# Attention backward: each dV product and each dK product also carries a transpose

## Chip, cores and metric

One core of one Trainium2 chip. The metric is the device time of one execution in microseconds; the kernel before takes 1630.79 us (median of 3 runs, 1629.3 to 1632.03).

## The reference

Two independent attention blocks A and B share the incoming gradient; the kernel computes the forward output and all gradients. B = 8 batches, Sq = 96 queries, H = 32 heads, Dh = 128, Sk = 512 cached keys, model width D = 640, all bf16.

```
def _A_ref(x, k_cache, v_cache, wq, wo):          # _B_ref is the same
    q = (x @ wq).reshape(B, Sq, H, Dh).transpose(0, 2, 1, 3)
    scores = jnp.einsum("bhqd,bhkd->bhqk", q, k_cache) * (Dh ** -0.5)
    p = softmax(scores, axis=-1)
    o = jnp.einsum("bhqk,bhkd->bhqd", p, v_cache)
    return o.transpose(0, 2, 1, 3).reshape(B, Sq, H * Dh) @ wo

def reference(..., grad_out):
    out, vjp = jax.vjp(concat(A, B), all ten inputs)
    return (out, *vjp(grad_out))   # dx, dk_cache, dv_cache, dwq, dwo of A and of B
```

Per head and batch: dV = P^T dO, dP = dO V^T, delta = rowsum(dO * O), dS = P * (dP - delta), dK = dS^T Q, dQ = dS K.

## The kernel before

The kernel is unrolled over blocks, heads and batches: 2 x 32 x 8 = 512 pairs of head and batch, and each pair passes through a software pipeline of "ticks", one pair entering per tick. Within a tick every stage stands in a slot; the list of (tick, slot) is sorted and emitted, and the framework's scheduler then fixes each engine's order, its buffers and its waits (`high_priority` moves the score path forward). One tick holds, each for another pair:

- s8 (`c_s8`): dQ^T in four products of 96 columns into `x_ps`, from `K_sb` and `dST_sb`; then, for the pair of s7, four transposes of dS into `dst_ps` (L349) and the DVE copy to `dST_sb` (L351).
- s7 (`c_s7`): dK in four products of 128 columns, `dS_sb` stationary and `Qnat_h` moving (L435), evacuated by ACT to `dK_sb` (L438).
- s5 and s4 (`c_s45`): O^T in four products into `x_ps` (L362), four transposes of P into `x_ps` (L368), ACT evacuations to `OD` (L378) and `PT_sb` (L381).
- s4 (`c_s4`): dV in four products, `P_sb` stationary and `dOnat_h` moving (L392), evacuated by ACT to `dV_sb` (L395).
- s6 (`c_s6`): dP (L420), the row sums delta as a product of `prod` and a column of ones into `dl_ps` (L422), and dS on DVE in one instruction (L424).
- s2, s3: scores `S_ps` (L301), their maximum on DVE (L303), exp on ACT (L313), reciprocal on DVE (L323), P on GpSimd (L332). s5b: `prod` on GpSimd (L410).

s4 to s8 of one pair follow each other tick by tick, so dST of a tick is read by dQ^T in the next, PT by O^T in the next, and dS by dK in the next.

Work by head (projections `q_ps` L246, transposes of weights, `n_ps` L261 for Q and dO in natural layout, `nat_ps` L458, weight gradients `dwo_ps` L472 and `dwq_ps` L493, output and dx products `o_ps` L517) is placed at the end of ticks, with evacuations on ACT or DVE through the helper `evac` (L160, L163, L165). SyncE issues the loads, the DMA transposes of K and V, and the stores.

PSUM has eight banks here, in one pool, and each tile takes one:

```
ps=P(name="ps", bufs=8, space=PSUM),
...
def bank(shape, dt, name):
    return ps.tile(shape, dt, name=name, tag="bank")
```

Of the kernel before, what the change touches and what calls it, by code (L numbers as in the profile page):

```python
# [7 lines left out]
ACT = mybir.ActivationFunctionType  # L8
ALU = mybir.AluOpType
AX = mybir.AxisListType  # L10
F32 = mybir.dt.float32
BF16 = mybir.dt.bfloat16
PSUM = bass.MemoryType.PSUM
# [33 lines left out]
OFF = dict(ldk=-5, ldv=-4, kt=-3, vt=0, s2=3, s3=3, s4=4, s5=5, s6=6, s7=7, s8=8)  # L47
HK = dict(pA=-10, pA2=-9, pB=-3, pC0=[-2, 0], pC1=[-1, 0], pD1=1, pD0=2, qA0=18, qA1=17, qA1e=21, qDw=(18, 29), qB=[19, 20], qD=[(18, 0, 2), (19, 2, 4), (21, 4, 5)])
EV = dict(pB0="act", pB1="dve", pC00="act", pC01="act", pC10="act", pC11="dve", pD0="dve", pD1="dve", qA0="act", qA1="dve", qB0="act", qB1="dve", qD="dve", gU="act")
# [4 lines left out]
SLOTS = dict(LOAD=0, S2A=5, S2B=5.5, S1=6, S8=10, S7=20, S5=30, S4=40, S6=50, S3A=52, S3B=53, S5B=54, HEAD=SL_HEAD, GRP=SL_GRP)  # L54


def build_block(tc, em, tick0, blk, x, kc, vc, wq, wo, g_all, out_all, dx, dk, dv, dwq, dwo, ident, ones, pools, HG=6, first=True, groups=None):
    nc = tc.nc
    B, Sq, D = x.shape
    _, H, Sk, Dh = kc.shape  # L60
# [40 lines left out]
    def bank(shape, dt, name):  # L101
        return ps.tile(shape, dt, name=name, tag="bank")
# [3 lines left out]
    SB = {}  # L106
# [51 lines left out]
    def evac(eng, dst, src, sc=None):  # L158
        if eng == "act":
            nc.scalar.activation(dst, src, ACT.Identity, scale=(1.0 if sc is None else sc))  # L160
        else:
            if sc is None:
                nc.vector.tensor_copy(dst, src)  # L163
            else:
                nc.vector.tensor_scalar(dst, src, float(sc), None, op0=ALU.mult)  # L165
# [84 lines left out]
    def pD(h, which):  # L250
        def f():
            st = HS[(blk, h)]
            src = st["QT_h"] if which == 0 else st["dOT_h"]
            dst = hd.tile([Sq, B * 128], BF16, name="Qnat_h" if which == 0 else "dOnat_h")
            st["Qnat_h" if which == 0 else "dOnat_h"] = dst
            for b0 in range(0, B, 8):
                nb = min(8, B - b0)
                n_ps = bank([Sq, 8 * 128], BF16, "n_ps")
                for i in range(nb):
                    b = b0 + i  # L260
                    nc.tensor.transpose(n_ps[:, i * 128:(i + 1) * 128], src[:, b * Sq:(b + 1) * Sq], ident[:])  # L261
                evac(EV["pD%d" % which], dst[:, b0 * 128:(b0 + nb) * 128], n_ps[:, 0:nb * 128])
        return f

    def c_ld(h, b, n, bufs):
# [70 lines left out]
    def c_s8(tick, k8, k7):  # L336
        def f():
            XP[tick] = bank([128, 1024], BF16, "x_ps")
            if k8 is not None:
                st = CS[(k8[0], k8[1], k8[2])]  # L340
                dQT_ps = XP[tick][:, 2 * Sq:4 * Sq].bitcast(F32)
                for c in range(KC):
                    nc.tensor.matmul(dQT_ps, st["K_sb"][:, c, :], st["dST_sb"][:, c * Sq:(c + 1) * Sq], start=(c == 0), stop=(c == KC - 1))  # L343
                del CS[(k8[0], k8[1], k8[2])]
            if k7 is not None:
                st7 = CS[(k7[0], k7[1], k7[2])]
                dST_ps = bank([128, KC * Sq], BF16, "dst_ps")
                for c in range(KC):
                    nc.tensor.transpose(dST_ps[:, c * Sq:(c + 1) * Sq], st7["dS_sb"][:, c * 128:(c + 1) * 128], ident[0:Sq, 0:Sq])  # L349
                dST_sb = wk.tile([128, KC * Sq], BF16, name="dST_sb", bufs=2)  # L350
                nc.vector.tensor_copy(dST_sb[:], dST_ps[:])  # L351
                st7["dST_sb"] = dST_sb
        return f

    def c_s45(tick, k8, k5, k4):
        def f():
            pt_ps = XP.pop(tick)
            if k5 is not None:
                st = CS[(k5[0], k5[1], k5[2])]
                OT_ps = pt_ps[:, 0:2 * Sq].bitcast(F32)  # L360
                for c in range(KC):
                    nc.tensor.matmul(OT_ps, st["V_sb"][:, c, :], st["PT_sb"][:, c * Sq:(c + 1) * Sq], start=(c == 0), stop=(c == KC - 1))  # L362
            if k4 is not None:
                st4 = CS[(k4[0], k4[1], k4[2])]
                P_sb = st4["P_sb"]
                PT_ps = pt_ps[:, 4 * Sq:4 * Sq + KC * Sq]
                for c in range(KC):
                    nc.tensor.transpose(PT_ps[:, c * Sq:(c + 1) * Sq], P_sb[:, c * 128:(c + 1) * 128], ident[0:Sq, 0:Sq])  # L368
            both = [(k, which) for which, k in enumerate((k5, k8)) if k is not None]
            if both:  # L370
                at = [(HS[(k[0], k[1])]["slot"], k[2] * Sq) for k, _ in both]
                v = OD[:, both[0][1], at[0][0], at[0][1]:at[0][1] + Sq]
                src = pt_ps[:, 2 * Sq * both[0][1]:2 * Sq * (both[-1][1] + 1)].bitcast(F32)
                if len(both) == 2:
                    step = (OD.shape[2] + at[1][0] - at[0][0]) * T + at[1][1] - at[0][1]
                    v = bass.AP(v.tensor, v.offset, [v.ap[0], (step, 2), (1, Sq)])
                    src = src.rearrange("p (a q) -> p a q", a=2)
                nc.scalar.activation(v, src, ACT.Identity, scale=1.0)  # L378
            if k4 is not None:
                PT_sb = wk.tile([128, KC * Sq], BF16, name="PT_sb", bufs=2)  # L380
                nc.scalar.activation(PT_sb[:], PT_ps, ACT.Identity, scale=1.0)  # L381
                st4["PT_sb"] = PT_sb
        return f

    def c_s4(h, b):
        def f():
            st = CS[(blk, h, b)]
            hs = HS[(blk, h)]
            P_sb = st["P_sb"]
            dV_ps = bank([128, KC * 128], F32, "dV_ps")  # L390
            for c in range(KC):
                nc.tensor.matmul(dV_ps[:, c * 128:(c + 1) * 128], P_sb[:, c * 128:(c + 1) * 128], hs["dOnat_h"][:, b * 128:(b + 1) * 128], start=True, stop=True)  # L392
            if b % 2 == 0:
                SB[(blk, h, b // 2, "v")] = wk.tile([128, 2, KC * 128], BF16, name="dV_sb", bufs=4)
            nc.scalar.activation(SB[(blk, h, b // 2, "v")][:, b % 2], dV_ps[:], ACT.Identity, scale=1.0)  # L395
        return f

    def c_st(h, b, which):
# [5 lines left out]
    def c_s5b(h, b):  # L404
# [6 lines left out]
            st["prod"] = prod  # L411
        return f

    def c_s6(h, b):
        def f():
            st = CS[(blk, h, b)]
            hs = HS[(blk, h)]
            tok = slice(b * Sq, (b + 1) * Sq)
            dP_ps = bank([Sq, Sk], F32, "dP_ps")
            nc.tensor.matmul(dP_ps[:], hs["dOT_h"][:, tok], st["VT"], start=True, stop=True)  # L420
            dl_ps = bank([Sq, 1], F32, "dl_ps")
            nc.tensor.matmul(dl_ps[:], st["prod"][:], ones[:, 0:1], start=True, stop=True)  # L422
            dS_sb = wk.tile([Sq, Sk], BF16, name="dS_sb", bufs=2)
            nc.vector.scalar_tensor_tensor(dS_sb[:], dP_ps[:], dl_ps[:, 0:1], st["P_sb"][:], op0=ALU.subtract, op1=ALU.mult)  # L424
            st["dS_sb"] = dS_sb
        return f

    def c_s7(h, b):
        def f():
            st = CS[(blk, h, b)]  # L430
            hs = HS[(blk, h)]
            dS_sb = st["dS_sb"]
            dK_ps = bank([128, KC * 128], F32, "dK_ps")
            for c in range(KC):
                nc.tensor.matmul(dK_ps[:, c * 128:(c + 1) * 128], dS_sb[:, c * 128:(c + 1) * 128], hs["Qnat_h"][:, b * 128:(b + 1) * 128], start=True, stop=True)  # L435
            if b % 2 == 0:
                SB[(blk, h, b // 2, "k")] = wk.tile([128, 2, KC * 128], BF16, name="dK_sb", bufs=4)
            nc.scalar.activation(SB[(blk, h, b // 2, "k")][:, b % 2], dK_ps[:], ACT.Identity, scale=1.0)  # L438
        return f

    def qA(h, which):
# [121 lines left out]
    for g in range(NG):  # L563
        h0 = GH0[g]
        for hh in range(groups[g]):
# [17 lines left out]
            for b in range(B):  # L583
# [14 lines left out]
                if b % 2 == 1:  # L598
                    em.add(ct + OFF["s4"] + 1, SLOTS["LOAD"] + 1.5, c_st(h, b, "v"))
                    em.add(ct + OFF["s7"] + 1, SLOTS["LOAD"] + 1.5, c_st(h, b, "k"))  # L600
                em.add(ct + OFF["s4"], SLOTS["S4"], c_s4(h, b))
                for i, o in enumerate(("s8", "s7", "s5", "s4")):
                    SX.setdefault(ct + OFF[o], [None] * 4)[i] = (blk, h, b)
                em.add(ct + OFF["s6"], SLOTS["S6"], c_s6(h, b))
                em.add(ct + OFF["s7"], SLOTS["S7"], c_s7(h, b))
            hk = HK if first or h < H - 1 else dict(HK, qA0=13, qB=[14, 15], qA1=16, qD=[(19, 0, 2), (19, 2, 4), (19, 4, 5)])
# [42 lines left out]
def _kernel_impl(tc, A_x, A_k_cache, A_v_cache, A_wq, A_wo, B_x, B_k_cache, B_v_cache, B_wq, B_wo, grad_out,  # L649
# [13 lines left out]
    with ExitStack() as ctx:  # L663
# [7 lines left out]
        nc.vector.memset(warm[:], 1.0)  # L671
        pools = dict(
            const=P(name="const", bufs=1),
            ps=P(name="ps", bufs=8, space=PSUM),
            kvp=P(name="kv", bufs=11),
            wk=P(name="wk", bufs=3),
            hd=P(name="hd", bufs=2),
# [7 lines left out]
        pools["SX"] = {}  # L685
        pools["XP"] = {}
        pools["OD"] = pools["const"].tile([128, 2, HG + 2, A_x.shape[0] * A_x.shape[1]], BF16, name="OD", bufs=1)
        pools["HS"] = {}
        pools["CS"] = {}
        em = Emitter()  # L690
# [77 lines left out]
```

## Time and profile before

| | |
|---|---|
| median of 3 runs | 1630.79 us |
| profiled execution | 1629.74 us, its span 1628.0 us |
| TensorE (PE) busy | 1605.0 us, 99% of the span, 20881 matmuls |
| TensorE weight loads (PEld) | 1286.4 us, 79% |
| VectorE (DVE) | 1269.9 us, 78% |
| ScalarE (ACT) | 1391.5 us, 85% |
| GpSimd (POOL) | 528.5 us, 32% |
| granted TensorE clock | 0.999 |
| DMA | 454.96 MB, mean 279 GB/s |

PE is the matmul stream, PEld the weight loads that run beside it. A group line of the profile gives line, engine, operation, what is written and read with shapes, the count, then busy time in us, mean ns of one, idle time before it and what ended that. A timeline line gives start and length in us. Matmuls are pipelined, so the length of one is not what it costs in a stream; the distance of starts is.

### The profile page before, as it was taken

Reading aid. Unit: us, or ns where it says so; the run is one execution under the profiler, and the core shown is the slowest. Engines: PE = TensorE matmul, PEld = TensorE weight load, DVE = VectorE, ACT = ScalarE, POOL = GpSimd, SP = SyncE. Lnnn points to the kernel's source line nnn. Section 1 sums busy time; section 2 is a strip of 40 time slices with the busy share of each in tenths; the row PEclk is TensorE's granted clock in tenths of the full one; section 3 lists DMA queues with packets and bytes.
Section 4 is the critical chain, followed back from the end, with each engine's and each line's share of the span. In section 5 each row is a group of like instructions: output and inputs, shape, how many; then the busy total and the mean of one; then the engine's idle time right before and its main releaser. Section 6 shows DMA issues by size and latency. Waiting matters only on the chain.

```text
span 1628.0 us, 55048 instructions
## 1 busy us (share of the span) xinstructions
PE 1605.0 (99%) x20881; PEld 1286.4 (79%) x21048; DVE 1269.9 (78%) x2907; ACT 1391.5 (85%) x3518; POOL 528.5 (32%) x1034
## 2 busy tenths in 40 slices
PE   8999999999999999999999999999999999999998
PEld 7887787787788787877878777877877877877876
DVE  6886687778788788788878767878878878777887
ACT  7999898798898797988879889978987977987984
POOL 2333333233333233333323323323333333332332
PEclk9999999999999999999999999999999999999999
DMA  9999999999999999999999999999999999999994
GB/s 268 284 290 293 274 292 285 278 275 289 283 281 287 274 282 278 272 277 299 277 303 287 285 285 286 283 294 277 276 295 268 294 288 266 283 274 285 287 280 142
DMA packets 875626, 454.96 MB, mean 279 GB/s; under 512 B 548192, under 2 KB 875360, under 8 KB 875360
## 3 DMA queue, kind: packets, MB, share of 16 engines
q1 hardware_dynamic: 875360, 451.43, 112.8%
q8 instruction: 165, 2.70, 0.7%
q14 instruction: 101, 0.83, 0.1%
HBM read 161.09 MB, written 159.12 MB: 197 GB/s over the span
## 4 chain that ended last, share of the span: by engine, by line
PE 93%; DVE 2%; ACT 2%; issue 1%; DMA 1%; SPq 0%; POOL 0%; DVEq 0%; ACTq 0%; POOLq 0%
PE q_ps L246 13%; PE o_ps L517 12%; PE dK_ps L435 7%; PE dV_ps L392 7%; PE dP_ps L420 7%; PE S_ps L301 7%; PE dwo_ps L472 6%; PE dwq_ps L493 6%; PE dst_ps L349 5%; PE x_ps L368 5%; PE x_ps L362 5%; PE x_ps L343 5%; PE n_ps L261 3%; PE nat_ps L458 3%; PE woT_ps L213 1%
## 5 line engine op out<-in xcount | busy, mean ns | idle before, releaser
L332 POOL TENSOR_SCALAR P_sb<-E_sb,rinv 96x512 bf16<-96x512 bf16 x512 | 354.2, 692 | 1072.2 <-DVE rinv L323 1038.4
L313 ACT ACTIVATE E_sb<-S_ps,negm 96x512 bf16<-96x512 f32 x512 | 356.3, 696 | 117.2 <-DVE negm L303 111.7
L424 DVE SCALAR_TENSOR_TENSOR dS_sb<-dP_ps,dl_ps,P_sb 96x512 bf16<-96x512 f32 x512 | 382.8, 748 | 43.6 <-PE dl_ps L422 36.6
L438 ACT ACTIVATE dK_sb<-dK_ps 128x512 bf16<-128x512 f32 x512 | 307.4, 600 | 84.8 <-PE dK_ps L435 83.8
L303 DVE TENSOR_REDUCE negm<-S_ps 96x1 f32<-96x512 f32 x512 | 347.6, 679 | 37.5 <-PE S_ps L301 36.4
L395 ACT ACTIVATE dV_sb<-dV_ps 128x512 bf16<-128x512 f32 x512 | 316.2, 618 | 0.0
L381 ACT ACTIVATE PT_sb<-x_ps 128x384 bf16<-128x384 bf16 x512 | 258.1, 504 | 0.0
L517 PEld LDWEIGHTS <-OD 128*128 128x128 bf16 x1536 | 135.3, 98 | 102.8 <-issue 2.0
L392 PE MATMUL dV_ps<-dOnat_h,P_sb 96*128 96x128 bf16 x2048 | 197.9, 219 | 0.6 <-DVE dOnat_h L163 0.6
L435 PE MATMUL dK_ps<-Qnat_h,dS_sb 96*128 96x128 bf16 x2048 | 198.0, 219 | 0.0
L420 PE MATMUL dP_ps<-VT,dOT_h 128*96 128x512 bf16 x512 | 195.3, 381 | 0.3
L323 DVE RECIPROCAL rinv<-rowsum 96x1 f32<-96x1 f32 x512 | 80.3, 157 | 144.8 <-ACT E_sb L313 141.5
L351 DVE COPY dST_sb<-dst_ps 128x384 bf16<-128x384 bf16 x512 | 177.7, 347 | 17.5 <-PE dst_ps L349 17.5
L410 POOL TENSOR_TENSOR prod<-OD,dOT_h 128x96 bf16<-128x96 bf16 x512 | 186.5, 364 | 8.8 <-ACT OD L378 8.2
L301 PE MATMUL S_ps<-KT,QT_h 128*96 128x512 bf16 x488 | 184.9, 379 | 0.4
L378 ACT ACTIVATE OD<-x_ps 128x192 bf16<-128x192 f32 (+1 forms) x515 | 173.3, 336 | 3.7 <-PE x_ps L343 3.7
L349 PE MATMUL dst_ps<-ident,dS_sb 96*128 96x96 bf16 x2048 | 172.4, 206 | 0.5 <-ACT PT_sb L381 0.3
L362 PE MATMUL x_ps<-PT_sb,V_sb 128*128 128x96 bf16 x2048 | 172.2, 206 | 0.2 <-ACT PT_sb L381 0.2
L368 PE MATMUL x_ps<-ident,P_sb 96*128 96x96 bf16 x2048 | 171.9, 205 | 0.6 <-POOL P_sb L332 0.3
L343 PE MATMUL x_ps<-dST_sb,K_sb 128*128 128x96 bf16 x2048 | 170.9, 206 | 0.0
L343 PEld LDWEIGHTS <-K_sb 128*128 128x128 bf16 x2048 | 135.3, 98 | 38.2
L493 PE MATMUL dwq_ps<-dQnat,x_nat 128*128 128x256 bf16 x960 | 142.7, 273 | 0.0
(75 smaller groups left out, 3042.5 us busy)
## 6 DMA issues: line engine op xcount, KB each, us to landing
out_dram<-dV_sb SPq DMA_DIRECT2D x256, 256.0 KB, 3.6
out_dram<-dK_sb SPq DMA_DIRECT2D x256, 256.0 KB, 3.5
K_sb<-in_A_k_cache_dram SPq DMA_DIRECT2D x128, 256.0 KB, 4.1
V_sb<-in_A_v_cache_dram SPq DMA_DIRECT2D x128, 256.0 KB, 3.9
K_sb<-in_B_k_cache_dram SPq DMA_DIRECT2D x128, 256.0 KB, 4.0
V_sb<-in_B_v_cache_dram SPq DMA_DIRECT2D x128, 256.0 KB, 4.0
out_dram<-dwo_sb SPq DMA_DIRECT2D x64, 160.0 KB, 3.2
out_dram<-dwq_sb SPq DMA_DIRECT2D x32, 320.0 KB, 4.2
```

Source lines behind the costliest of these rows:

```text
L301: nc.tensor.matmul(S_ps[:], hs["QT_h"][:, tok], st["KT"], start=True, stop=True)
L303: nc.vector.tensor_reduce(negm[:], S_ps[:], axis=AX.X, op=ALU.max, negate=True)
L313: nc.scalar.activation(E_sb[:], st["S_ps"][:], ACT.Exp, bias=st["negm"][:], scale=1.0, accum_out=rowsum[:])
L332: pinned(nc.gpsimd.tensor_scalar(P_sb[:], st["E_sb"][:], st["rinv"][:], 0.0, op0=ALU.mult, op1=ALU.add))
L343: nc.tensor.matmul(dQT_ps, st["K_sb"][:, c, :], st["dST_sb"][:, c * Sq:(c + 1) * Sq], start=(c == 0), stop=(c == KC - 1))
L392: nc.tensor.matmul(dV_ps[:, c * 128:(c + 1) * 128], P_sb[:, c * 128:(c + 1) * 128], hs["dOnat_h"][:, b * 128:(b + 1) * 128], start=True, s ...
L395: nc.scalar.activation(SB[(blk, h, b // 2, "v")][:, b % 2], dV_ps[:], ACT.Identity, scale=1.0)
L420: nc.tensor.matmul(dP_ps[:], hs["dOT_h"][:, tok], st["VT"], start=True, stop=True)
L424: nc.vector.scalar_tensor_tensor(dS_sb[:], dP_ps[:], dl_ps[:, 0:1], st["P_sb"][:], op0=ALU.subtract, op1=ALU.mult)
L435: nc.tensor.matmul(dK_ps[:, c * 128:(c + 1) * 128], dS_sb[:, c * 128:(c + 1) * 128], hs["Qnat_h"][:, b * 128:(b + 1) * 128], start=True, s ...
L438: nc.scalar.activation(SB[(blk, h, b // 2, "k")][:, b % 2], dK_ps[:], ACT.Identity, scale=1.0)
L517: nc.tensor.matmul(o_ps[:], src[:, t * 128:(t + 1) * 128], rhs, start=(hh == 0), stop=(hh == groups[g] - 1))
```

## The change

The four transposes of P and the four dV products have the same stationary operand, a chunk of P; likewise dS and dK. The change puts the 96 x 96 identity beside dO (and beside Q) in the moving operand, so that one product of 224 columns gives the chunk of dV and the chunk of P transposed (and of dK and dS transposed). Two batches share one row of 128 + 96 + 128 columns, [dO of the even batch | identity | dO of the odd batch], so an even batch reads [dO | I] and an odd one [I | dO]. Four chunks of 224 fp32 columns need two banks; the eight banks become four single ones and two pairs. delta goes into the last column of the pair that dV uses in that tick, and is emitted ahead of dV. The natural layouts of dO and Q are no longer tiles by head but rotating places in `DN` (8 rows of two batches) and `QN` (6 rows). `c_s8` and `c_s45` lose the transposes and the copies to `dST_sb` and `PT_sb`; these copies move to `c_s7` (DVE) and `c_s4` (ACT). `c_s7` changes as `c_s4` does, with `QN` and a pair of banks of its own.

```diff
-            dst = hd.tile([Sq, B * 128], BF16, name="Qnat_h" if which == 0 else "dOnat_h")
+            dst = pools["DN" if which else "QN"]
+            n_pairs = dst.shape[1]
+            p0 = (blk * H + h) * (B // 2)
...
-                evac(EV["pD%d" % which], dst[:, b0 * 128:(b0 + nb) * 128], n_ps[:, 0:nb * 128])
+                lo = 0
+                while lo < nb // 2:
+                    at = (p0 + b0 // 2 + lo) % n_pairs
+                    n = min(nb // 2 - lo, n_pairs - at)
+                    v = dst[:, at, 0:128]
+                    v = bass.AP(v.tensor, v.offset, [v.ap[0], (128 * 2 + Sq, n), (128 + Sq, 2), (1, 128)])
+                    evac(EV["pD%d" % which], v, n_ps[:, lo * 256:(lo + n) * 256].rearrange("p (a b d) -> p a b d", b=2, d=128))
+                    lo += n
...
     def c_s4(h, b, tick):
...
-            dV_ps = bank([128, KC * 128], F32, "dV_ps")
+            W = 128 + Sq
+            dV_ps = wide(tick)
+            rhs = pools["DN"][:, ((blk * H + h) * (B // 2) + b // 2) % pools["DN"].shape[1], (b % 2) * 128:(b % 2) * 128 + W]
             for c in range(KC):
-                nc.tensor.matmul(dV_ps[:, c * 128:(c + 1) * 128], P_sb[:, c * 128:(c + 1) * 128], hs["dOnat_h"][:, b * 128:(b + 1) * 128], start=True, stop=True)
+                nc.tensor.matmul(dV_ps[:, c // 2, (c % 2) * W:(c % 2 + 1) * W], P_sb[:, c * 128:(c + 1) * 128], rhs, start=True, stop=True)
+            both = dV_ps[:, :, 0:2 * W].rearrange("p a (c w) -> p a c w", w=W)
+            o_dv, o_pt = (0, 128) if b % 2 == 0 else (Sq, 0)
+            PT_sb = wk.tile([128, KC * Sq], BF16, name="PT_sb", bufs=2)
+            nc.scalar.activation(PT_sb[:].rearrange("p (a c q) -> p a c q", a=2, c=2), both[:, :, :, o_pt:o_pt + Sq], ACT.Identity, scale=1.0)
...
-            nc.scalar.activation(SB[(blk, h, b // 2, "v")][:, b % 2], dV_ps[:], ACT.Identity, scale=1.0)
+            nc.scalar.activation(SB[(blk, h, b // 2, "v")][:, b % 2].rearrange("p (a c d) -> p a c d", a=2, c=2), both[:, :, :, o_dv:o_dv + 128], ACT.Identity, scale=1.0)
...
+    def wide(tick):
+        if tick not in pools["WP"]:
+            pools["WP"][tick] = pools["psw"].tile([128, 2, 512], F32, name="dV_ps", tag="wide")
+        return pools["WP"][tick]
+
+    def c_dl(h, b, tick):
+        def f():
+            st = CS[(blk, h, b)]
+            st["dl_ps"] = wide(tick)[0:Sq, 1, 511:512]
+            nc.tensor.matmul(st["dl_ps"], st["prod"][:], ones[:, 0:1], start=True, stop=True)
+        return f
...
-            dl_ps = bank([Sq, 1], F32, "dl_ps")
-            nc.tensor.matmul(dl_ps[:], st["prod"][:], ones[:, 0:1], start=True, stop=True)
+            dl_ps = st["dl_ps"]
...
+            dK_ps = pools["psw"].tile([128, 2, 512], F32, name="dK_ps", tag="wide")
...
+            nc.vector.tensor_copy(dST_sb[:].rearrange("p (a c q) -> p a c q", a=2, c=2), both[:, :, :, o_st:o_st + Sq])
...
+                em.add(ct + OFF["s6"], SLOTS["S4"] - 1, c_dl(h, b, ct + OFF["s6"]))
...
-            ps=P(name="ps", bufs=8, space=PSUM),
+            ps=P(name="ps", bufs=4, space=PSUM),
+            psw=P(name="psw", bufs=2, space=PSUM),
...
+        for name, n in (("DN", Bn), ("QN", 3 * Bn // 4)):
+            pools[name] = pools["const"].tile([Sqn, n, 2 * 128 + Sqn], BF16, name=name, bufs=1)
+            for j in range(n):
+                nc.gpsimd.tensor_copy(pools[name][:, j, 128:128 + Sqn], ident[0:Sqn, 0:Sqn])
```

## The prediction

> **What bounds the kernel now.** I read the page first (busy shares, then the chain that ended last), then the timeline of one step, then the groups by form, and last the order in which the changed program's instructions stand on each engine.
>
> ```profile
> PE 1605.0 (99%) x20881; PEld 1286.4 (79%) x21048; DVE 1269.9 (78%) x2907; ACT 1391.5 (85%) x3518; POOL 528.5 (32%) x1034
> ...
> PE 93%; DVE 2%; ACT 2%; issue 1%; DMA 1%; SPq 0%; POOL 0%; DVEq 0%; ACTq 0%; POOLq 0%
> ```
>
> TensorE is busy 99% of the span and carries 93% of the chain. Whether it streams or is held up inside that busy time is seen in the PE rows of the timeline:
>
> ```profile
> 803.91 0.33 PE L343 MATMUL x_ps<-dST_sb,K_sb 128*128 128x96 bf16 x4
> 804.08 0.34 PE L349 MATMUL dst_ps<-ident,dS_sb 96*128 96x96 bf16 x4
> 804.25 0.39 PE L435 MATMUL dK_ps<-Qnat_h,dS_sb 96*128 96x128 bf16 x4
> 804.48 0.34 PE L362 MATMUL x_ps<-PT_sb,V_sb 128*128 128x96 bf16 x4
> 804.65 0.34 PE L368 MATMUL x_ps<-ident,P_sb 96*128 96x96 bf16 x4
> 804.82 0.39 PE L392 MATMUL dV_ps<-dOnat_h,P_sb 96*128 96x128 bf16 x4
> 805.04 0.38 PE L420 MATMUL dP_ps<-VT,dOT_h 128*96 128x512 bf16 x1
> 805.26 0.17 PE L422 MATMUL dl_ps<-ones,prod 128*96 128x1 bf16 x1
> ```
>
> Read start to start: four products of 96 columns take 0.17 us (42 to 43 ns each), four of 128 take 0.22 to 0.23 (56 each), one of 512 takes 0.22. All follow columns/2.4 ns + 2.4 ns. Summing that over all matmuls in the program gives 1572.6 us of a span of 1628.0. So TensorE streams nearly without a stall: 55.4 us are all that is left for the start (first dense stretch, about 11), the tail after the last matmul (4.1) and small waits. The profiled execution took 1629.74 (1.7 around the span); the median of the runs is 1630.79, 1.05 above it. A measurement of this kernel can tell about 0.2%, 3.3 us.
>
> **What the merged products save.** They take away 4096 transposes of 96 columns (L349, L368) with their weight loads, and lengthen 4096 products (L392, L435) from 128 to 224 columns, which the same line puts at 95.7 ns. The streamed columns stay the same; only 2.4 ns of each removed matmul go: 4096 x 2.4 = 9.8 us, and TensorE's work falls to 1562.8. (Some transposes start 46 instead of 42 ns apart; with their mean, 43.5, the saving would be 14. I take 9.8.)
>
> The removed weight loads are worth nothing by this: the PEld rows run beside the matmuls, and L349's and L368's groups start 42 ns apart although a load shows 98 ns. The Trainium skill, TensorE: Matmul & The Clock Gate, Back-to-back issue gap, says otherwise: a stream of load and product pairs sustains about 81 ns a pair at 128 columns. By an estimate from that figure the removed pairs would be worth several times my 9.8 us. The trace disagrees: 56 ns a pair at 128 columns.
>
> **What it adds off TensorE.** dST_sb is now copied from fp32 in PSUM instead of bf16:
>
> ```profile
> L351 DVE COPY dST_sb<-dst_ps 128x384 bf16<-128x384 bf16 x512 | 177.7, 347 | 17.5 <-PE dst_ps L349 17.5
> ...
> L163 DVE CAST dwo_sb<-dwo_ps 128x320 bf16<-128x320 f32 x64 | 30.9, 483 | 0.7
> ...
> L163 DVE CAST dOT_h<-q_ps 128x256 bf16<-128x256 f32 x64 | 26.7, 417 | 10.0 <-PE q_ps L246 10.0
> ```
>
> The fp32 rows rise 66 ns for 64 columns, so 384 columns cost 483 + 66 = 549 ns, 0.2 us more than L351: DVE's busy time grows by 104 us to 1374, still under TensorE's work, so it costs nothing as throughput. ACT's evacuations keep their element counts and its rate (384 columns 504 ns, 512 fp32 columns 600 to 618), so I take no change; slower strided reads could only add. The scatter into DN and QN (677 ns each, 64 + 64 times, a third of QN's in two pieces) and the 14 copies of the identity on idle POOL lie beside TensorE's work: nothing, at most 4 us at the start for POOL.
>
> **A new wait in the step's own loop.** Before, dS (L424) waited for TensorE alone, and dl_ps had a bank of its own. Now dl is a column of the bank pair that holds dV and P's transpose, and in the changed program dS waits for ACT: in the order with its waits it is released by the dV_sb evacuation of the same pair. In the same way ACT's dK_sb now waits for DVE's dST copy. The Trainium skill, PSUM — Partial Sum Buffer, PSUM bank collisions raise a hardware error, says that two engines may not touch one bank in the same quarter of the partitions at once, even when both read. By that rule the wait cannot go while dl sits in that bank. No trace of before shows two readers of one bank.
>
> So dK of the next step waits for: last dV product, PT_sb, often dK_sb, dV_sb, dS. Prices:
>
> ```profile
> 804.85 0.58 ACT L438 ACTIVATE dK_sb<-dK_ps 128x512 bf16<-128x512 f32 x1
> ...
> 805.33 0.32 ACT L378 ACTIVATE OD<-x_ps 128x192 bf16<-128x192 f32 x1
> ...
> 805.50 0.75 DVE L424 SCALAR_TENSOR_TENSOR dS_sb<-dP_ps,dl_ps,P_sb 96x512 bf16<-96x512 f32 x1
> 805.54 0.49 ACT L381 ACTIVATE PT_sb<-x_ps 128x384 bf16<-128x384 bf16 x1
> ...
> 805.91 0.60 ACT L395 ACTIVATE dV_sb<-dV_ps 128x512 bf16<-128x512 f32 x1
> ```
>
> A product ends 0.163 after its issue slot (219 less 56 ns), a handover takes about 0.05 (dl ends at 805.43, dS starts at 805.50; ACT is the same on other rows), PT_sb to dV_sb is 0.37 start to start, a dK_sb between them adds 0.48 (804.85 to 805.33), dV_sb takes 0.618, dS 0.748. Sum: 0.163 + 0.05 + 0.37 + 0.618 + 0.05 + 0.748 + 0.04 = 2.04 us, or 2.52 with dK_sb between, which is so in 376 of 510 steps of ACT's order. Against that stands what TensorE has to do between that dV and the dK: summed in its new order by the issue line, 1.6 us at the 5th percentile, 2.07 at the median, 2.8 at the 90th. 356 of the 510 steps fall short, by 193.5 us together. TensorE executes in order: behind the waiting dK stand dl, dV, dP and the work of the heads.
>
> **Half the banks for the rest.** Before, 4383 PSUM tiles rotate through 8 banks: one bank serves a tile every 1628/548 = 3.0 us. After, dV and dK use two pairs, and the other 2839 tiles (S, x_ps, dP, and everything by head) have 4 banks: every 2.3 us. For each wait of TensorE on ACT or DVE in the new order I took the evacuation that releases it, the product that feeds that, and TensorE's work between product and waiter; what is needed is the evacuation's own duration + 0.27 us (0.163 and two handovers). Example: 73 dP products wait for the OD evacuation (338 ns), and in 59 the OT product that feeds it is the matmul just before: 0.61 us of standstill each. Others are S_ps, x_ps and o_ps waiting for evacuations of a head, with 0.2 to 0.7 us of work between. Shortfalls: 541 places, 165.1 us, with time already lost between counted once. The same count on the order of before gives 7.7 us: its 8 banks do hide this.
>
> **Sum.** Both together, lost time counted once: 279.8 us. Carried over from before: 55.4 - 7.7 = 47.7. Span 1562.8 + 47.7 + 279.8 = 1890, execution 1892, if ACT and DVE are always free when called. They are not: exp (0.66 start to start), its reduction (0.68) and evacuations of the heads (0.4 to 0.8) stand in the same queues. With 0.1 us more for each release the loss is 342.7 us, with 0.2 407.0, with 0.3 475.0. On the order of before 0.2 more gives 19.3 and 0.4 gives 49.6, where at most 55.4 - 15 = 40 are there, so more than 0.3 is excluded. I take 0.1, low in that span, because ACT's share falls to 1391/1955 = 71%: 1562.8 + 47.7 + 342.7 + 1.7 = 1955.
>
> **Rivals.**
> *Only one of the two holds*, because the other's releasers come earlier than priced (ACT takes dV_sb before dK_sb, say). Banks alone 1562.8 + 47.7 + 165.1 + 1.7 = 1777; the loop alone 1806. For it: they overlap in time, so the first pays part of the second. Against: the orders are fixed and each is 160 us or more by itself. Chance 0.17.
> *Queues cost more*, 0.3 us a release: 2087 and above. For it: the timeline shows dV's evacuation begin 1.1 us after dV's first product (804.82 to 805.91). Chance 0.1.
> *All waits are hidden*, TensorE keeps streaming: 1629.7 - 9.8 = 1620, faster. One mechanism decides: the release of dS. If the way from dV to dS were 1.75 us for every step, the loop would lose 10.9 us and cancel the saving; below that, and with bank releases as early, the change gains. Against: evacuation and dS alone, 0.618 + 0.748, leave 0.38 for product, handovers and PT_sb. Chance 0.04.
> *Weight loads set the pace*, and 4096 fewer shorten the span by up to the busy time of the two groups: 116.2 + 116.1 = 232, to 1397. This is what the skill's page of TensorE would favour. The 42 ns spacing speaks against it: chance 0.01.
> That the change doesn't do what it says is excluded by the order: the transposes are gone, and 512 wide dK and dV products stand there.
>
> **Numbers.** The forecast, both mechanisms with 0 to 0.2 us of queueing (1892 to 2019), has 0.68. The range takes in the banks-alone case and 0.3 us of queueing: 1777 to 2087. Faster 0.04 + 0.01, no change 0.01 (losses that happen to cancel 9.8), slower 0.94.
>
> **What would show it.** Right: PE's busy share falls to 80 to 88%; the waits name dS_sb by ACT dV_sb, dK_ps products by DVE dS_sb, and S_ps, dP_ps, x_ps and o_ps products by ACT and DVE evacuations; dK_ps starts in the timeline 96 ns apart within a group and rarely under 2.8 us from step to step (before: 2.4 at the 5th percentile, 3.0 at the median); dST_sb at 549 ns. Wrong: PE at 97% or more, or dS still waiting for PE; then my prices or the overlap of the two are too high, and the 9.8 us remain.

## The result, and the profile after

The changed kernel takes 2017.22 us (median of 3 runs, 2016.68 to 2017.25), 1.2369 times the kernel before (95% interval 1.2352 to 1.2386). The profiled span is 2015.4 us, 387.4 more than before, although TensorE's work by the issue line is 9.8 us less.

The changed kernel's page, busy times and the chain that ended last:

```profile
PE 1746.9 (87%) x16952; PEld 1277.5 (63%) x16952; DVE 1413.9 (70%) x2928; ACT 1436.7 (71%) x3518; POOL 531.2 (26%) x1048
...
PE 43%; ACT 34%; DVE 12%; issue 8%; DMA 2%; POOL 1%; ACTq 0%; SPq 0%; DVEq 0%; POOLq 0%
```

No engine is full any more. The chain, which was TensorE's for 93%, now goes through ACT and DVE for 46%. How it goes is in the chain in order of time of the changed kernel (start, length, what), over one step:

```profile
808.38 0.56 PE dK_ps L445 x4
808.94 0.01 PE dV_ps L420
808.95 0.41 PE dV_ps L384 x4
809.35 0.23 PE dP_ps L429
...
809.61 0.19 ACT E_sb L321
809.80 0.38 ACT PT_sb L388
810.17 0.49 ACT dV_sb L392
810.67 0.03 issue
810.69 0.76 DVE dS_sb L432
811.45 0.04 issue
811.50 0.33 PE x_ps L351 x4
811.83 0.39 PE dK_ps L445 x4
```

This is the loop: dK, dV, PT_sb, dV_sb, dS, dK, and again. A row of the chain begins where the chain enters a group, which can be after the group's own start. The starts of the dK products stand in the timeline of TensorE:

```profile
808.38 0.56 PE L445 MATMUL dK_ps<-QN,dS_sb 96*128 96x224 bf16 x4
...
811.66 0.55 PE L445 MATMUL dK_ps<-QN,dS_sb 96*128 96x224 bf16 x4
```

From one dK to the next it takes 811.66 - 808.38 = 3.28 us in this step, in which ACT works on E_sb ahead of PT_sb and on dK_sb after dV_sb. The release of dS also frees the bank of dP for x_ps (811.50), so part of the loop's loss appears at x_ps. Over the whole trace the distance from one step's first dK product to the next was 2.41 us at the 5th percentile, 2.67 at the 25th and 3.03 at the median; it is now 3.36, 3.49 and 3.70. Short steps, which had kept the mean low, are gone, and the long ones have grown too (95th percentile 4.03 before, 4.81 now).

The list of waits of the changed kernel (who waited for whom, us in total, times, longest):

```profile
DVE dS_sb L432 <- ACT dV_sb L392: 186.3, 250, 1.8
...
PEld L445 <- DVE dS_sb L432: 148.0, 221, 1.2
PEld L351 <- issue: 117.8, 272, 1.1
PEld L532 <- issue: 50.8, 101, 1.6
...
PE dP_ps L429 <- ACT E_sb L321: 44.7, 69, 1.0
...
PE dP_ps L429 <- ACT OD L372: 28.0, 65, 0.6
```

A weight load stands just ahead of its product, so a wait for data is shown at PEld: 148.0 us of dK's loads wait for dS. The dP rows are waits for a bank: nothing that dP reads comes from E_sb or OD. Where the rows say "issue" the profile names no releaser. Worked out from the starts instead (the part of each start-to-start distance beyond the issue line, where it is over 30 ns, put down to the product that starts late), TensorE stands 431 us in the changed kernel: 122 at dP, 100 at x_ps, 55 at S_ps, 54 at o_ps, 43 at dK, 57 elsewhere. These are the places that the prediction named. The rows of dST_sb and of a wide product, groups by form:

```profile
L449 DVE CAST dST_sb<-dK_ps 128x384 bf16<-128x384 f32 x512 | 283.0, 553 | 104.9 <-PE dK_ps L445 61.6 <-PE dV_ps L420 36.2
...
L384 PE MATMUL dV_ps<-DN,P_sb 96*128 96x224 bf16 x2048 | 282.4, 257 | 0.8 <-DVE DN L163 0.6 <-POOL P_sb L340 0.2
```

### The profile page after: what moved, and what is told of

The parts are those of the page before. It is cut to its first block, busy times and chain, and to the rows that moved or that the text cites. A ratio compares the mean times of both kernels' runs of the same rounds, so it can differ in the third digit from the quotient of the medians.

```text
span 2015.4 us, 47828 instructions
## 1 busy us (share of the span) xinstructions
PE 1746.9 (87%) x16952; PEld 1277.5 (63%) x16952; DVE 1413.9 (70%) x2928; ACT 1436.7 (71%) x3518; POOL 531.2 (26%) x1048
## 4 chain that ended last, share of the span: by engine, by line
PE 43%; ACT 34%; DVE 12%; issue 8%; DMA 2%; POOL 1%; ACTq 0%; SPq 0%; DVEq 0%; POOLq 0%
ACT E_sb L321 9%; PE dK_ps L445 8%; ACT dK_sb L453 8%; PE dV_ps L384 7%; ACT dV_sb L392 6%; ACT PT_sb L388 6%; PE o_ps L532 5%; DVE dS_sb L432 5%; PE dP_ps L429 4%; DVE negm L311 4%; PE x_ps L351 3%; PE S_ps L309 3%; PE q_ps L246 3%; PE x_ps L362 2%; ACT OD L372 2%
## 5 line engine op out<-in xcount | busy, mean ns | idle before, releaser
L432 DVE SCALAR_TENSOR_TENSOR dS_sb<-dP_ps,dV_ps,P_sb 96x512 bf16<-96x512 f32 x512 | 383.7, 749 | 200.7 <-ACT dV_sb L392 186.3
L388 ACT ACTIVATE PT_sb<-dV_ps 128x384 bf16<-128x384 f32 x512 | 249.1, 487 | 163.6 <-PE dV_ps L384 157.5
L449 DVE CAST dST_sb<-dK_ps 128x384 bf16<-128x384 f32 x512 | 283.0, 553 | 104.9 <-PE dK_ps L445 61.6
L453 ACT ACTIVATE dK_sb<-dK_ps 128x512 bf16<-128x512 f32 x512 | 302.4, 591 | 26.9 <-DVE dST_sb L449 26.7
L392 ACT ACTIVATE dV_sb<-dV_ps 128x512 bf16<-128x512 f32 x512 | 307.5, 601 | 0.0
L445 PE MATMUL dK_ps<-QN,dS_sb 96*128 96x224 bf16 x2048 | 288.6, 260 | 20.2 <-DVE dS_sb L432 17.7
L384 PE MATMUL dV_ps<-DN,P_sb 96*128 96x224 bf16 x2048 | 282.4, 257 | 0.8 <-DVE DN L163 0.6
L445 PEld LDWEIGHTS <-dS_sb 96*128 96x128 bf16 x2048 | 172.4, 97 | 160.7 <-DVE dS_sb L432 148.0
L384 PEld LDWEIGHTS <-P_sb 96*128 96x128 bf16 x2048 | 162.6, 97 | 2.1 <-issue 0.9
L532 PE MATMUL o_ps<-wqT_h,OD 128*128 128x128 bf16 (+1 forms) x768 | 133.1, 301 | 32.3 <-ACT woT_h L160 7.3
L532 PE MATMUL o_ps<-wo_h,OD 128*128 128x128 bf16 (+1 forms) x768 | 136.3, 299 | 7.5 <-DVE dwq_sb L165 2.1
```

The costliest lines, as they stand in the source:

```text
L384: nc.tensor.matmul(dV_ps[:, c // 2, (c % 2) * W:(c % 2 + 1) * W], P_sb[:, c * 128:(c + 1) * 128], rhs, start=True, stop=True)
L388: nc.scalar.activation(PT_sb[:].rearrange("p (a c q) -> p a c q", a=2, c=2), both[:, :, :, o_pt:o_pt + Sq], ACT.Identity, scale=1.0)
L392: nc.scalar.activation(SB[(blk, h, b // 2, "v")][:, b % 2].rearrange("p (a c d) -> p a c d", a=2, c=2), both[:, :, :, o_dv:o_dv + 128], AC ...
L445: nc.tensor.matmul(dK_ps[:, c // 2, (c % 2) * W:(c % 2 + 1) * W], dS_sb[:, c * 128:(c + 1) * 128], rhs, start=True, stop=True)
L449: nc.vector.tensor_copy(dST_sb[:].rearrange("p (a c q) -> p a c q", a=2, c=2), both[:, :, :, o_st:o_st + Sq])
L453: nc.scalar.activation(SB[(blk, h, b // 2, "k")][:, b % 2].rearrange("p (a c d) -> p a c d", a=2, c=2), both[:, :, :, o_dk:o_dk + 128], AC ...
```

## The experiments

Theory: the loss has two parts that each cost time by themselves, the loop through the pair that dV and delta share, and four banks for work that had eight. Rivals: the loop alone, the banks alone, or the wide products themselves (fp32 copy, evacuation of dK behind it). Each kernel was timed in turns with the kernel before on the same chip; the ratios are to that.

**The loop taken out, banks and wide products kept.**

```diff
-            nc.vector.scalar_tensor_tensor(dS_sb[:], dP_ps[:], dl_ps[:, 0:1], ...
+            nc.vector.scalar_tensor_tensor(dS_sb[:], dP_ps[:], pools["zero"][0:Sq, 0:1], ...
```

> The changed kernel, but dS takes its scalar from a column of zeros in SBUF, so delta is left out of dS; its product is still issued. dS then waits for dP alone and no longer for the evacuation of dV; the four banks, the pairs and the wide products stay. If the loop (dV product, PT_sb, dV_sb, dS, dK) and the four banks each cost about what the prediction says by themselves, 1780 to 1840 us remain. If the loop is nearly all of it and the bank waits come mostly from the order that the scheduler built around it, 1650 to 1740 (in the new order of this kernel the bank shortfalls sum to 57 us with prompt releases and 129 with 0.2 us more each). If the banks are nearly all of it, 1950 to 2020.

Measured 1706.12 us, ratio 1.0472 (1.0454 to 1.0490). Without the loop 311 of the 387 us are gone. From the view of the tile dS_sb in the changed kernel, DVE's idle time before dS by what ended it, and the longest of those who waited for dS (us, times):

```profile
  ACT dV_sb L392: 186.3, 250
...
  PEld L445: 148.0, 221
```

and in this one, where dS idles only for dP and dK's loads no longer wait:

```profile
  PE dP_ps L429: 27.6, 95
...
  PEld L445: 1.5, 4
```

1706 lies in the range of "the loop is nearly all of it". But 76 us stay, so it is not the whole.

**The loop put into the kernel before.**

```diff
+            dl_sb = wk.tile([Sq, 1], F32, name="dl_sb", bufs=2)
+            nc.scalar.activation(dl_sb[:], dl_ps[:], ACT.Identity, scale=1.0)
-            nc.vector.scalar_tensor_tensor(dS_sb[:], dP_ps[:], dl_ps[:, 0:1], ...
+            nc.vector.scalar_tensor_tensor(dS_sb[:], dP_ps[:], dl_sb[:, 0:1], ...
```

> The kernel before with its eight banks, its separate transposes and products, and only this added: ACT copies delta from PSUM to a column in SBUF behind dV_sb in its queue, and dS reads that column. So dS waits for the same place in ACT's queue as in the changed kernel, with no shortage of banks and no wide products; ACT gets 512 instructions of about 0.2 us. If the loop costs time by itself: 92 us short with prompt releases in its order (dK_sb stands between in 223 of 510 steps), 148 with 0.2 us more each, so 1720 to 1780. If the banks alone make the loss: 1630 to 1650.

Measured 1847.98 us, ratio 1.1336 (1.1320 to 1.1353): +218, above the expected 92 to 148. Its waits:

```profile
DVE dS_sb L426 <- ACT dl_sb L424: 247.3, 275, 1.7
...
PEld L349 <- DVE dS_sb L426: 186.9, 300, 1.7
PE dst_ps L349 <- DVE dS_sb L426: 139.2, 244, 1.5
```

dst_ps is the first reader of dS here, and TensorE stands there (PE and PEld rows overlap in time, so they aren't added). With eight banks the loop is enough for more than half of the loss. Worked out from the starts as above, TensorE stands 197 us at dst_ps, which is most of the 218. The copy of delta, 180 ns at the median, stands in this loop and not in that of the changed kernel; what ACT's 512 extra copies cost without a reader was not run.

**The banks alone.**

```diff
-            ps=P(name="ps", bufs=8, space=PSUM),
+            ps=P(name="ps", bufs=4, space=PSUM),
+            psw=P(name="psw", bufs=4, space=PSUM),
```

`dV_ps`, `dK_ps`, `dst_ps` and `dl_ps` take the four banks of `psw`.

> The kernel before with its eight banks split as the change splits them: four for S, x_ps, dP and the tiles of the heads, four single ones for dV, dK, dst_ps and dl_ps. No wide products, no new wait of dS. If the four banks cost time by themselves as predicted (165 us or more): 1790 or more. By the shortfalls in its own new order: 81 us with prompt releases, 150 with 0.2 more, 1700 to 1770. If the loop alone makes the loss: 1630 to 1650.

Measured 1779.01 us, ratio 1.0917 (1.0899 to 1.0935): +149 with no wide product and no new wait of dS, 9 us above the expected 1770.

**One bank fewer.** `bufs=7` in the kernel before, nothing else.

> The kernel before with seven banks instead of eight, all shared, nothing else changed: 626 tiles a bank instead of 548. If the kernel before has no bank to spare: 1651 to 1699 (29 and 77 us of shortfalls in its order). If eight banks were ample and only the four of the changed kernel are short: 1630 to 1640.

Measured 1677.31 us, ratio 1.0295 (1.0278 to 1.0312): +47. Its page still shows TensorE as full:

```profile
span 1675.2 us, 55140 instructions
...
PE 1644.7 (98%) x21048; PEld 1297.2 (77%) x21048; DVE 1283.9 (77%) x2907; ACT 1398.8 (84%) x3518; POOL 526.8 (31%) x1034
```

The kernel before had no bank to spare.

**Both suspects together, without wide products.** The edits of the loop and of the banks in one kernel.

> The two suspects together without any wide product: the kernel before with its banks split four and four, and with ACT's copy of delta behind dV_sb, which dS reads. Alone they gave +149 and +218 us. If these two make the loss of the changed kernel: 1950 to 2050, near the sum 1997. If they share their waits: 1850 to 1900, and then something else in the wide products is needed for 2017.

Measured 1964.83 us, ratio 1.2056 (1.2038 to 1.2074): +335, near the sum of the two alone (218 + 149 = 367). So 335 of the 387 us appear with the transposes and products as they were, in a loop that also holds the copy of delta. The other 52 (62, as the changed kernel has 9.8 us less work) must lie in what the two kernels don't share; one candidate is dK_sb between PT_sb and dV_sb in ACT's queue, in 376 of 512 steps of the changed kernel's trace against 194 in this one's. That wasn't tried apart.

**DVE's longer copy.**

```diff
                 nc.vector.tensor_copy(dST_sb[:], dST_ps[:])
+                again = wk.tile([128, Sq], BF16, name="again", bufs=2)
+                nc.vector.tensor_copy(again[:], dST_ps[:, 0:Sq])
```

> The kernel before with one more DVE instruction a step, right behind the copy of dst_ps: 96 of its columns copied once more, about 198 ns, which is what the fp32 copy adds in the changed kernel (206 ns). Nothing reads it. The prediction took this for nothing as throughput: 1630 to 1640. If DVE's queue is part of the loss: 1650 to 1700.

Measured 1636.14 us, ratio 1.0033 (1.0020 to 1.0046): +6 (3 to 7 by the interval) for 193 ns a step on DVE. In the kernel before it is nearly hidden.

**The wide product with fewer banks.** The half with dK alone: c_s7, `QN` and its identity as in the change, `bufs=6` for the rest and one pair for dK. Beside it the same split of banks without a wide product: six shared, two single ones for dK and dst_ps.

> Half of the change: only dK carries the transpose of dS, with one pair of banks for it; dV, the transposes of P and delta are as in the kernel before and share the six other banks with the rest. No wait of dS for dV_sb. If the loop through dV and the four banks are what cost: 1667 to 1715 us by the shortfalls of its order (50 and 98 us; 3359 tiles on 6 banks are 560 a bank, against 548 before and 710 in the changed kernel). If the wide product itself, its fp32 copy on DVE or the evacuation of dK behind that copy is what costs: about half of the loss, 1800 or more. If only the wait of dS costs: 1625.

> The kernel before with its banks split as in the half with dK alone: six shared, two single ones for dK and dst_ps; separate transposes and products, the bf16 copy of dst_ps on DVE as before. The half with dK alone took 1716. If its loss of 86 us is due to the banks: 1676 to 1723 (54 and 101 us of shortfalls). If it is due to the wide product, its fp32 copy (553 instead of 347 ns) or dK_sb waiting behind that copy: 1630 to 1650.

Measured 1716.02 (ratio 1.0530, 1.0513 to 1.0548) for the half, 1 above its expected range, and 1755.97 (1.0773, 1.0757 to 1.0790) for the split alone, 33 above. So the loss of the half needs no wide product. At that split the wide product is 40 us faster than four transposes and four products. TensorE's work explains 4.9 of it. Whether the rest is the order, or that one pair released together serves better than two single banks in turn, stays open. The half with dV alone was not run.

**Moving things in the step.** The changed kernel, `S7=45` for `S7=20`, so that dK stands behind dV:

> The changed kernel with one number changed: slot S7 = 45 instead of 20, so that dK with its transpose stands behind dV in TensorE's step instead of ahead of it. dS still waits for dV_sb and the banks stay four and two pairs, but dV of a step no longer stands behind a dK that waits for dS of the step before: the loop no longer closes. In its order TensorE has 3.0 us of work at the median between dV and the dK that needs it (2.07 in the changed kernel), and 3 steps of 510 fall short. If the closed loop costs what the prediction says: 1710 to 1810 (98 to 195 us of bank shortfalls remain). If the wait of dS as such costs the time, or the banks do: 1950 or more.

Measured 1813.44, ratio 1.1125 (1.1108 to 1.1142): 3 above its expected range. 204 us come back though dS still waits for dV_sb, so most of the cost came with the closing of the loop and not with that wait as such. The move does more than open the loop, though: in ACT's queue dK_sb no longer stands between PT_sb and dV_sb in any step, and on the half with dK alone, which has no loop through dV_sb, the same move gives 22 us (below). No run parts these. The list of its waits shows what remains of it and what is new:

```profile
PEld L420 <- POOL prod L407: 82.9, 157, 1.2
DVE dS_sb L432 <- ACT dV_sb L392: 74.0, 161, 0.7
...
PE dV_ps L420 <- POOL prod L407: 43.0, 87, 1.0
```

dV's products stand behind delta on TensorE, and delta now waits for prod on GpSimd. Then delta in a free column of x_ps (the x_ps of the tick), with dK in its old place:

```diff
-            st["dl_ps"] = wide(tick)[0:Sq, 1, 511:512]
+            st["dl_ps"] = pools["XD"][tick][0:Sq, 1022:1024].bitcast(F32)
-                em.add(ct + OFF["s6"], SLOTS["S4"] - 1, c_dl(...))
+                em.add(ct + OFF["s6"], SLOTS["S5"] - 1, c_dl(...))
```

> The changed kernel with delta put into a free column of x_ps instead of the pair that dV uses, and emitted ahead of O^T. dS then waits for the OD evacuation of x_ps, which stands ahead of PT_sb and dV_sb in ACT's queue, so the way from dV to dS is gone without leaving delta out; the x_ps bank is held until dS has read it. If the loop through dV_sb is what costs: 1744 to 1843 us by the shortfalls in its order (131 us with prompt releases, 231 with 0.2 more), more than without delta (1706) because x_ps is held longer and dS waits for OD. If any wait of dS for ACT costs as much as the one for dV_sb: 1950 or more.

Measured 1816.23, ratio 1.1146 (1.1130 to 1.1163), inside the expected range: 201 us come back with delta in place.

**Looking for a faster version.** The half with dK alone and `S7=45`, and the same with delta in x_ps:

> The half with dK alone, and slot S7 = 45: dK behind dV in the step. By the shortfalls of its order 12 us with prompt releases, 39 with 0.2 more: 1629 to 1656, that is the kernel before or slightly above. If the place of dK is without effect where dS does not wait for dV_sb: as the half alone.

> As the one before, and delta in a free column of x_ps, which takes 512 tiles off the six banks (474 a bank). dS waits for PT_sb, the last reader of x_ps. Shortfalls 13 and 31 us: 1630 to 1648. It beats the kernel before only if releases are as prompt as priced: TensorE's work is 4.9 us less. If a wait of dS for ACT costs by itself: above the one before by 20 or more.

Measured 1693.56 (1.0391, 1.0376 to 1.0407) and 1714.28 (1.0518, 1.0503 to 1.0534). Both miss: the counts of shortfalls gave 1629 to 1656 and 1630 to 1648. dK late gains 22 on the half, and delta in x_ps loses 21. A loss of 20 or more was the sign set for "a wait of dS for ACT costs by itself", but the trace puts it elsewhere: TensorE idles about 2 us in all for dS, and stands 41 us (from the starts) at the product of delta, which now comes earlier and waits for prod. From the view of the delta product's line, what it waited for:

```profile
  POOL prod L417: 49.1, 139
```

No version here beats the kernel before.

## Why the prediction was right, and where a size was off

- *What bounds the kernel, and the issue line.* Right. The four wide products of a dK start 96 ns apart at the median (predicted 95.7), and no transposes are left. The saving in work is there and too small to be seen. Of the signs that were named, TensorE's busy share (87%), dS waiting for dV_sb and the spacing came.
- *Removed weight loads are worth nothing.* Right by the spacing: each group of products keeps to the issue line, before with the 4096 loads and after without them. In the total time a small gain from them could not be told beside this loss. The Trainium skill's 81 ns a pair (TensorE: Matmul & The Clock Gate, Back-to-back issue gap) is in none of these runs; pairs of 128 columns start 56 ns apart in the kernel before.
- *The fp32 copy.* Its size was right (549 predicted, 553 measured), and taking it for nothing was right to 6 us by the run with a longer DVE step. DVE's busy time came to 1413.9 us and not 1374, because its rows overlap less (added up they grow by 110 us, 105 of it dST_sb). The run with the longer step has the nearly wait-free order of before; in the changed kernel dST_sb also releases dK_sb (26.7 us of ACT's waits), which was not priced.
- *The loop.* Right, and shown from both sides: 311 us fall away without it, 218 come with it alone. The predicted loop of 2.52 us from dV to dK plus dK, delta and dV themselves gives 3.33; in the 376 steps of the trace that have dK_sb between PT_sb and dV_sb, one dK follows the last by 3.36 us at the 5th percentile and 3.45 at the median. Without dK_sb the price was 2.04, or 2.85 for the round, and that was too low: in 94 of the 136 other steps dK_sb stands just ahead of PT_sb instead. The rule that forces the wait (the Trainium skill, PSUM — Partial Sum Buffer, PSUM bank collisions raise a hardware error) agrees with the order, where dS waits for the last ACT reader of the pair. No run lets two engines read one bank at once, so what would happen is not shown.
- *Half the banks.* Right in kind: +149 with the split alone, +47 with one bank less. The 4383 tiles were counted short: 2839 and 512 each of dV, dK, dst_ps and dl_ps make 4887, so a bank served a tile every 2.7 us before, not 3.0, against 2.3 after. The expectations carry the same short count. The shortfalls were counted wait by wait and don't rest on it. The 541 shortfalls of 165 us in the changed kernel's order were partly the scheduler's answer to the loop: without the loop the whole arrangement of four banks and two pairs loses 76 net of the saving.
- *The term that was mis-sized* is the queueing of releases, taken as 0.1 us. Span less TensorE's work is 2015.4 - 1562.8 = 452.6; less the 47.7 carried over it is 405, against 342.7 predicted and 407.0 in the row for 0.2 us. That this row fits doesn't show that each release cost 0.2. One release can be read from the trace: by the prices PT_sb starts 0.31 us after the start of the last dV product (0.096 of issue, 0.163 and 0.05), and it starts 0.29 us a step later than that on average, 151 us over 512 steps, 78 of them in the 94 steps with dK_sb ahead of it (not all of that need be lost time). The reason for going low, a smaller share of ACT, was wrong: at 71% busy its queue still holds dK_sb, E_sb and OD where PT_sb is due. That fits a time at the upper end of the forecast (1892 to 2019). The same bias shows in the experiments: of the ten ranges made from such counts seven were passed at the upper end, by 1 to 68 us.
- *Rivals.* One of the two alone is refuted: each costs over 100 us by itself in the kernel before. Queues at 0.3 us a release, 2087 and above, are 70 us too dear. Hidden waits and a pace set by weight loads are refuted by the span.

## What to carry to other kernels

When a kernel fills an engine, its buffers are part of the tuning: ask of a merge how many banks it takes from the other tiles before asking how many instructions it saves. Two results in one bank tied their readers together here; write down the round from one step's product to the next step's through every reader of that bank, and compare it with the shortest step, not the mean. Price each release with the queue it stands in, by what stands ahead of it and not by the engine's load: at 71% PT_sb still began 0.29 us late on average.

## What the hardware showed that was not expected

TensorE's busy share hardly tells a standstill of this size. With seven banks it reads 98% where 47 us are lost, and without delta 97% (1645.2 of 1704.0) where the work by the issue line is 1562.8: a product shows 219 to 260 ns while it occupies 56 to 96 of issue, so its end covers the gap behind it. Here the sum of columns/2.4 + 2.4 ns per product, set against the span, showed the loss. The standstills, up to 1.6 us in the list of PE's and PEld's waits, did not lower the granted clock: 0.998 in the changed kernel, 0.999 before.
